# A new order for the first stage of a fused attention and MoE kernel: set-up products moved, C loaded without its zeros, the second weight tile sent for later

## The chip, the cores and the metric

The kernel runs on one core of one Trainium2 chip. The metric is the device time of one launch in microseconds (us), the median of several runs. TensorE (PE) multiplies matrices, VectorE (DVE), ScalarE (ACT) and GpSimd (POOL) work on elements, SyncE (SP) only starts transfers here. Each engine takes its instructions in the order in which the program wrote them; they wait for each other by semaphores.

## The reference

Three parts follow each other. First, a chunked linear attention over 4 batches, 8 heads, 768 positions, head size 32, state size 16:

```python
cum = np.cumsum(log_a, axis=-1)                 # per chunk of 32
L = np.exp(cum[..., :, None] - cum[..., None, :]) * causal
y_intra = einsum('bhij,bhjd->bhid', einsum('bhin,bhjn->bhij', C, B) * L, x)
y_inter = einsum('bhin,bhnd->bhid', C, state) * exp(cum)
state = exp(sum log_a) * state + sum_j B_j x_j exp(cum_end - cum_j)
```

Its output, 3072 tokens by 256, goes through a gated MLP (`silu(x @ w_gate) * (x @ w_val) @ w_out`, 1536 wide) and then through a routed MoE of 8 experts (256 to 1024 to 256, one expert for each token, with a gate).

## The kernel before

The attention is cut into 24 units (`NU`) of 128 positions by all 8 heads of a batch; four units make a block of 512 tokens. A product in full precision is made of three products of split operands (high by high, high by low, low by high), so most tensors have a high and a low half.

For a unit, `load(u)` (L160) sends for x, B and the transposed B in one tile (`xbb`, 256 KB) and for C in another (`cbd`, 256 KB, L170). The C tile is block diagonal over four heads: in each row three of four blocks of 64 columns are zeros, which come from memory with the rest. `weigh(u)` (L273) multiplies x by decays W; `scores_mm(u)` (L281) makes the state products (L291) and the scores (L297); `scores_m(u)` (L301, L305) masks the scores on VectorE; `states(u)` (L308) steps the running state on VectorE and ScalarE; `values_mm(u)` (L331) makes the outputs (L343, L353); `values_out(u)` (L357) multiplies them by the table `U` on VectorE and casts them on ScalarE into the high half of `xt` (L374); `values_low(u)` (L376) makes the low half (L380).

The decays are built once for each two blocks. `setup_ln` (L178) takes logarithms, `setup_decay` (L184, product `pw`) makes W, `setup_cum` (L189, product `pe`) makes `er`, `cum_split` (L218) splits it; `cum_ends_d`, `cum_ends` (L228, L236, product `pe2` with the table of ones `r16`) and `cum_store` make `eb`; `emit_d` (L249) spreads `er` into `du` on GpSimd (L259), and `emit_u` (L264) multiplies `du` by the table of ones `r32` (product `pu`, L270) and copies the result to `U` on ScalarE (L271). `setup_ones` (L213) casts the two tables from the constants `c1`.

The weights of the MLP come as 12 tiles (`load_w`, L387, 768 KB each, in three buffers, so that a tile can be sent for when the tile three before it has been read). They arrive as 64-bit floats and are decoded to a high half `wh` and a low half `wl` by `decode(f, ...)` (L396): parts 0 and "t" on ScalarE (L403, L406), "b" and "c" on VectorE (L412, L416), 2 on ScalarE (L419, `wh`), 3 on VectorE or GpSimd (L421, `wl`).

`first_block` (L807) writes the order of the first stage by hand, for all engines. After the set-up it runs units 0 to 3 in a loop, with pieces of decoding between them and `keep_busy` products (L199, L204), whose result nobody reads, behind each unit. Then a loop over i = 0 to 23 runs the MLP's products for the first two blocks (`mlp1_mm`, L430, 12 products of 128x512 for each i), with units 4 to 11 and the decoding of tiles 2 to 11 between them by two tables (`todo`, `units`). The first of these products needs all four units of block 0 and tile 0. The rest of the kernel is a loop over the further blocks with the routing, and the tiles of the experts.

SP's queue holds nearly all loads in program order: one that has to wait for its buffer holds up those behind it. The constants `c1` are sent for on ScalarE's queue.

## Time and profile before

| what | value |
|---|---|
| median of 3 runs | 530.3 us (530.1 to 530.32) |
| the profiled execution: its own time, its span | 530.17 us, 528.4 us |
| TensorE busy over the span | 505.0 us (96%), 4580 products |
| VectorE, ScalarE, GpSimd busy | 289.1, 219.5, 105.8 us |
| granted TensorE clock, mean | 0.989 |
| moved by DMA | 45.55 MB, mean 86 GB/s |

The span runs from the first to the last instruction. Busy times say how long an engine worked, not whether somebody waited for it; for that the chain of waits follows the work that ended last back to the start. The lines L... are those of the kernel before. In a timeline the bracket names how long the engine had been idle before an instruction, and what released it; "issue" stands for time in which it waited for nothing that the profile shows.

### The profile page before, as it was taken

How to read it: one execution, taken by the hardware profiler on the slowest of the kernel's cores; microseconds unless marked ns; L12 is line 12 of the kernel's file. 1: busy time of each engine (PE TensorE's matmuls, PEld its weight loads, DVE VectorE, ACT ScalarE, POOL GpSimd, SP SyncE). 2: the span in 40 equal slices, each digit the busy share in tenths (PEclk: the TensorE clock that was granted, in tenths of full speed). 3: DMA queues.
4: the chain of work that ended last, by engine and by line, in shares of the span. 5: the costliest groups of instructions: out<-in, count | busy, mean ns of one | idle time of the engine just before them, and what ended most of it. 6: DMA issues, size and time to landing. Idle time of an engine off the chain costs nothing.

```text
span 528.4 us, 11243 instructions
## 1 busy us (share of the span) xinstructions
PE 505.0 (96%) x4580; PEld 416.7 (79%) x4580; DVE 289.1 (55%) x631; ACT 219.5 (42%) x403; POOL 105.8 (20%) x127
## 2 busy tenths in 40 slices
PE   6889999999999999999999999999999999999990
PEld 3677787778788778888788778888899989999880
DVE  4998786944554544445444554455466564646320
ACT  4785575434333334233333332434454353534220
POOL 3200000220220130005000224211055426240220
PEclk9999999999999999999999999999999999999995
DMA  8954422011230312012100104234188544521100
GB/s 299 338 183 137 155 80 82 25 49 41 82 32 30 103 15 66 3 47 74 21 2 2 43 1 158 84 121 41 41 105 176 162 130 137 153 104 42 40 22 22
DMA packets 20694, 45.55 MB, mean 86 GB/s; under 512 B 4768, under 2 KB 8352, under 8 KB 20640
## 3 DMA queue, kind: packets, MB, share of 16 engines
q1 hardware_dynamic: 17424, 38.29, 26.2%
q0 software_dynamic: 3072, 6.41, 4.1%
q8 instruction: 37, 0.61, 0.6%
q14 instruction: 17, 0.14, 0.1%
q10 hardware_dynamic: 144, 0.11, 0.1%
HBM read 38.30 MB, written 6.50 MB: 85 GB/s over the span
## 4 chain that ended last, share of the span: by engine, by line
PE 76%; issue 11%; DVE 4%; POOL 3%; ACT 2%; DMA 1%; SPq 0%; POOLq 0%; DVEq 0%; ACTq 0%
PE py L469 19%; PE pg L441 18%; PE pv L441 18%; PE ph L758 7%; PE po L779 6%; PE pt L553 2%; POOL out L793 2%; PE pc L297 2%; PE py L353 1%; PE py L343 1%; PE pc L291 1%; DMA xbb<-in_xbb 1%; PE pu L270 1%; DVE wv L412 1%; PE px L747 1%
## 5 line engine op out<-in xcount | busy, mean ns | idle before, releaser
L441 PE MATMUL pg<-xt,wh 128*128 128x512 f32 x288 | 93.2, 404 | 0.3 <-ACT xt L374 0.2
L441 PE MATMUL pv<-xt,wh 128*128 128x512 f32 x288 | 90.4, 395 | 0.0
L449 DVE TENSOR_TENSOR h<-h,pv 128x512 f32<-128x512 f32 x72 | 49.4, 686 | 66.7 <-PE pv L441 55.6
L456 DVE TENSOR_TENSOR hl<-h,hh 128x512 fp32r<-128x512 f32 x72 | 50.2, 697 | 61.7 <-ACT hh L455 61.5
L758 PE MATMUL ph<-xt,hl 128*128 128x512 f32 x288 | 72.7, 394 | 0.0
L779 PE MATMUL po<-hl,hh 128*128 128x256 f32 x384 | 70.1, 283 | 0.0
L441 PEld LDWEIGHTS pv<-xt,wh 128*128 128x128 f32 x288 | 54.2, 188 | 12.8
L779 PEld LDWEIGHTS po<-hl,hh 128*128 128x128 f32 x384 | 60.3, 188 | 2.1
L455 ACT CAST hh<-h 128x512 fp32r<-128x512 f32 x72 | 44.6, 620 | 40.4 <-DVE h L449 40.4
L441 PEld LDWEIGHTS pg<-xt,wh 128*128 128x128 f32 x288 | 52.1, 188 | 11.6 <-ACT xt L374 0.6
L448 ACT ACTIVATE h<-pg 128x512 f32<-128x512 f32 x72 | 42.7, 593 | 41.7 <-PE pg L441 41.7
L614 POOL DMA_INDIRECT slots<-ids,si x24 | 26.0, 1081 | 168.4 <-DVE si L606 163.6
L758 PEld LDWEIGHTS ph<-xt,hl 128*128 128x128 f32 x288 | 51.7, 188 | 9.2
L469 PE MATMUL py<-hh,wh 128*128 128x512 f32 x144 | 58.7, 407 | 0.0
L441 PE MATMUL pg<-xt,wl 128*128 128x512 f32 x144 | 57.0, 396 | 0.3 <-DVE wl L421 0.3
L469 PE MATMUL py<-hl,wh 128*128 128x512 f32 x144 | 56.9, 395 | 0.0
L469 PE MATMUL py<-hh,wl 128*128 128x512 f32 x144 | 56.8, 394 | 0.0
L441 PE MATMUL pv<-xt,wl 128*128 128x512 f32 x144 | 56.8, 394 | 0.0
L779 PE MATMUL po<-hl,hl 128*128 128x256 f32 x192 | 53.9, 281 | 0.2 <-DVE hl L767 0.2
L767 DVE SCALAR_TENSOR_TENSOR hl<-ph,hh 128x512 fp32r<-128x512 f32 x48 | 33.0, 688 | 31.8 <-ACT hh L766 30.8
L766 ACT ACTIVATE hh<-ph 128x512 fp32r<-128x512 f32 x48 | 28.8, 600 | 41.4 <-PE ph L758 24.3
L779 PEld LDWEIGHTS po<-hl,hl 128*128 128x128 f32 x192 | 36.1, 188 | 0.4 <-DVE hl L767 0.4
(140 smaller groups left out, 669.6 us busy)
## 6 DMA issues: line engine op xcount, KB each, us to landing
eraw<-in_ew SPq DMA_DIRECT2D x24, 512.0 KB
wraw<-in_mw SPq DMA_DIRECT2D x12, 768.0 KB
xbb<-in_xbb SPq DMA_DIRECT2D x24, 256.0 KB
cbd<-in_cbd SPq DMA_DIRECT2D x24, 256.0 KB
yd<-yr SPq DMA_DIRECT2D x6, 528.0 KB
slots<-ids,si POOLq DMA_INDIRECT x24
xg<-yd,idx POOLq DMA_INDIRECT x24
out<-ob,idx POOLq DMA_INDIRECT x24
```

Source lines behind the costliest of these rows:

```text
L297: nc.tensor.matmul(out=r["pc"][g][32 * q:32 * q + 32, 0:256], lhsT=r["bt"][k, 32 * q:32 * q + 32], rhs=r["c"][k, q // 2].rearrange("p h i ...
L441: nc.tensor.matmul(out=t, lhsT=w[:, f, o:o + 128], rhs=xt[:, xp, k, cs], start=n == 0, stop=n == 5)
L448: nc.scalar.activation(out=h, in_=p[0], func=AF.Silu)
L449: nc.vector.tensor_tensor(out=h, in0=h, in1=p[1], op=ALU.mult)
L455: nc.scalar.copy(out=hh, in_=h)
L456: e.tensor_tensor(out=hl, in0=h, in1=hh.bitcast(F32), op=ALU.subtract)
L469: nc.tensor.matmul(out=yb[b][d][:, c:c + m], lhsT=w[:, f, o:o + 128], rhs=h, start=first and n == 0, stop=last and n == 2, skip_group_chec ...
L614: i = nc.gpsimd.indirect_dma_start(out=slots[0:E * upto], out_offset=bass.IndirectOffsetOnAxis(ap=si[:, s:s + 1], axis=0), in_=ids[g][:, o ...
L758: nc.tensor.matmul(out=p, lhsT=self.hl[:, w, o:o + 128], rhs=self.xt[:, xp, k], start=n == 0, stop=n == 5)
L766: nc.scalar.activation(out=hh, in_=p, func=AF.Relu)
L767: nc.vector.scalar_tensor_tensor(out=hl, in0=p, scalar=0.0, in1=hh.bitcast(F32), op0=ALU.max, op1=ALU.subtract)
L779: nc.tensor.matmul(out=self.po[s // 2][:, s % 2], lhsT=h[:, q], rhs=self.hl[:, w, o:o + DM], start=f == 0 and n == 0 and s % 2 == 0, stop= ...
```

## The change

C is loaded without half of its zeros: the rows of two heads are interleaved (`bk`, `bt`, C and the ones in `r16` get a new order), so that each row of a C tile needs only 256 of its 512 columns from memory. The tiles are four fixed buffers that GpSimd fills with zeros once, and each load writes two halves of 64 rows by 1 KB, in two transfers. The products read the tile with a stride; their number and size stay. In the first stage `setup_ones`, `cum_ends_d` and `emit_d(0)` come earlier; `warm_up` adds nine products of zeros in bf16 (five, two, two); the `keep_busy` products are 2, 2, 4, 4 instead of 0, 4, 4, 6. Unit 3's loads move to ScalarE's queue, behind `emit_u(0)`; the second weight tile is sent for behind unit 4, the third behind units 5 and 6. `emit_u(1)` moves from unit 0 to unit 2. The decoding of tiles 0, 1 and 2 is spread anew, tile 0's low half is made on VectorE instead of GpSimd, and unit 6's `weigh` comes before the MLP's loop.

```diff
--- before.py
+++ after.py
@@ -87,15 +87,16 @@
     at = inp["a"].reshape(NB * NH, NC, 128).reshape(NB, NH, NC, 128).transpose(3, 0, 2, 1)
     o["at"] = at.reshape(128, NBLK, 32)
     xk = inp["x"].reshape(NB, NH, NC, 128, D).transpose(3, 0, 2, 1, 4).reshape(128, NU, DM)
-    bk = inp["B"].reshape(NB, NH, NC, 128, N).transpose(3, 0, 2, 1, 4).reshape(128, NU, 128)
-    bt = inp["B"].reshape(NB, NH, NC, 128, N).transpose(1, 4, 0, 2, 3).reshape(128, NU, 128)
+    bq = inp["B"].reshape(NB, 4, 2, NC, 128, N)
+    bk = bq.transpose(4, 0, 3, 1, 5, 2).reshape(128, NU, 128)
+    bt = bq.transpose(1, 5, 2, 0, 3, 4).reshape(128, NU, 128)
     o["xbb"] = np.concatenate([xk, bk, bt], axis=2)
 
-    ct = inp["C"].reshape(NB, 2, 4, NC, 2, 64, N).transpose(1, 2, 6, 0, 3, 4, 5).reshape(2, 4, N, NU, 2, 64)
-    cd = np.zeros((2, 4, N, NU, 2, 4, 64), np.float32)
-    for h in range(4):
-        cd[:, h, :, :, :, h] = ct[:, h]
-    o["cbd"] = cd.reshape(128, NU, 512)
+    ct = inp["C"].reshape(NB, 2, 2, 2, NC, 128, N).transpose(1, 2, 6, 3, 0, 4, 5).reshape(2, 2, N, 2, NU, 128)
+    cd = np.zeros((2, 2, N, 2, NU, 2, 128), np.float32)
+    for p in range(2):
+        cd[:, p, :, :, :, p] = ct[:, p]
+    o["ct"] = cd.reshape(128, NU, 256)
     o["cst"] = _consts()
 
     def bits(w):
@@ -150,6 +151,7 @@
     r16 = ap_.tile([128, 128], F32R, name="r16")
     r32 = ap_.tile([128, 2, 128], F32R, name="r32")
     mk = c1[:, C_MK:C_MK + 64]
+    cbd = [ap_.tile([128, 4, 2, 64], F32, name=f"cbd{i}") for i in range(4)]
     raw = {}
     xt_t = {}
     y_t = {}
@@ -157,23 +159,34 @@
     v_t = {}
     s_t = {}
 
-    def load(u):
-        if u >= NU or u in raw:
-            return
-        r = {}
-        xbb = ap_.tile([128, 512], F32, name="xbb", tag="xbb", bufs=4)
-        nc.sync.dma_start(out=xbb, in_=I["xbb"][:, u])
-        r["x"] = xbb[:, 0:DM].rearrange("k (h d) -> k h d", h=8)
-        r["b"] = xbb[:, DM:DM + 128]
-        r["bt"] = xbb[:, DM + 128:]
-        r["c"] = ap_.tile([128, 2, 4, 64], F32, name="cbd", tag="cbd", bufs=4)
-        nc.sync.dma_start(out=r["c"].rearrange("p r h i -> p (r h i)"), in_=I["cbd"][:, u])
-        raw[u] = r
+    def load(*units, e=nc.sync, order=None):
+
+        t = []
+        for u in units:
+            if u >= NU or u in raw:
+                continue
+            r = raw[u] = {}
+            xbb = ap_.tile([128, 512], F32, name="xbb", tag="xbb", bufs=4)
+            r["x"] = xbb[:, 0:DM].rearrange("k (h d) -> k h d", h=8)
+            r["b"] = xbb[:, DM:DM + 128]
+            r["bt"] = xbb[:, DM + 128:]
+            r["c"] = cbd[u % 4]
+            t.append((xbb, I["xbb"][:, u]))
+            t.append((r["c"].rearrange("(r t) a c i -> t r (a c i)", t=2),
+                      I["ct"][:, u].rearrange("(r t) j -> t r j", t=2)))
+        for i in order or range(len(t)):
+            if i % 2:
+                for h in range(2):
+                    e.dma_start(out=t[i][0][h, :, 256 * h:256 * h + 256], in_=t[i][1][h])
+            else:
+                e.dma_start(out=t[i][0], in_=t[i][1])
 
     def setup_loads():
         nc.sync.dma_start(out=at0[:, 0:2], in_=I["at"][:, 0:2])
         nc.scalar.dma_start(out=c1, in_=I["cst"][:, 0:C1])
         nc.scalar.preload_act_table_set("natural_log_exp_and_others")
+        for t in cbd:
+            nc.gpsimd.memset(t, 0.0)
 
     def setup_ln(b0, b1):
         a = at[:, b0:b1]
@@ -205,14 +218,28 @@
                              rhs=r32.rearrange("p g j -> p (g j)").unsqueeze(1).to_broadcast([128, 2, 256]),
                              start=True, stop=True)
 
+    warm_t = []
+
+    def warm_up(n):
+
+        if not warm_t:
+            warm_t.append(ap_.tile([128, 128], BF16, name="zb"))
+            nc.vector.memset(warm_t[0], 0.0)
+            idle_t.append(ps.tile([128, 2, 256], F32, tag="y0", bufs=1, name="pi"))
+        for _ in range(n):
+            nc.tensor.matmul(out=idle_t[0].rearrange("p g j -> p (g j)").rearrange("p (n j) -> p n j", n=4),
+                             lhsT=warm_t[0], rhs=warm_t[0].unsqueeze(1).to_broadcast([128, 4, 128]),
+                             start=True, stop=True)
+
     def silu_first():
 
         t = ap_.tile([128, 1], F32, name="sf")
         nc.scalar.activation(out=t, in_=c1[:, C_ME:C_ME + 1], func=AF.Silu)
 
     def setup_ones():
+        p8 = c1[:, C_P8:C_P8 + 8].rearrange("p (q t) -> p q t", q=4).unsqueeze(2)
+        nc.vector.tensor_copy(out=r16.rearrange("p (q n t) -> p q n t", q=4, t=2), in_=p8.to_broadcast([128, 4, 16, 2]))
         p8 = c1[:, C_P8:C_P8 + 8].unsqueeze(2)
-        nc.vector.tensor_copy(out=r16.rearrange("p (h n) -> p h n", h=8), in_=p8.to_broadcast([128, 8, 16]))
         nc.vector.tensor_copy(out=r32.rearrange("p g (h i) -> p (g h) i", h=4), in_=p8.to_broadcast([128, 8, 32]))
 
     def cum_split(b0, n):
@@ -295,7 +322,7 @@
             for g in range(2):
                 k = slice(64 * g, 64 * g + 64)
                 nc.tensor.matmul(out=r["pc"][g][32 * q:32 * q + 32, 0:256], lhsT=r["bt"][k, 32 * q:32 * q + 32],
-                                 rhs=r["c"][k, q // 2].rearrange("p h i -> p (h i)"), start=True, stop=True,
+                                 rhs=r["c"][k, :, q // 2], start=True, stop=True,
                                  tile_position=(64 * g, 32 * q))
 
     def scores_m(u):
@@ -418,8 +445,8 @@
             elif part == 2:
                 nc.scalar.copy(out=wh[:, f], in_=wv_t[f].bitcast(F32))
             else:
-                low.tensor_tensor(out=wl[:, f], in0=wv_t.pop(f).bitcast(F32), in1=wh[:, f].bitcast(F32),
-                                  op=ALU.subtract)
+                nc.vector.tensor_tensor(out=wl[:, f], in0=wv_t.pop(f).bitcast(F32), in1=wh[:, f].bitcast(F32),
+                                        op=ALU.subtract)
 
 
     HALF = NF // 2
@@ -812,29 +839,33 @@
         nc.sync.dma_start(out=at0[:, 2:], in_=I["at"][:, 2:])
         load(2)
         load_w(0)
-        load(3)
-        load_w(1)
+        warm_up(5)
         setup_ln(0, 2)
+        setup_ones()
         setup_decay(0, 2)
         setup_cum(0, 1)
+        warm_up(2)
         weigh(0, nc.vector)
         scores_mm(0)
         cum_split(0, 1)
-        setup_ones()
+        p = cum_ends_d(0, 1)
+        d = emit_d(0)
         weigh(1, nc.gpsimd)
-        d = emit_d(0)
-        p = cum_ends(0, 1, cum_ends_d(0, 1))
+        p = cum_ends(0, 1, p)
+        warm_up(2)
         scores_m(0)
         cum_store(0, 1, p)
         states(0)
         emit_u(0, d)
+        load(3, e=nc.scalar)
         cum_pairs(1, 8)
         setup_ln(2, NBLK)
-        decode(0, 0)
         d = emit_d(1)
         weigh(2, nc.gpsimd)
         for u in range(4):
             scores_mm(u + 1)
+            if u == 2:
+                emit_u(1, d)
             values_mm(u)
             if u == 1:
                 setup_decay(2, NBLK)
@@ -842,38 +873,43 @@
             if u < 3:
                 scores_m(u + 1)
                 states(u + 1)
-            if u in (0, 2):
-                decode(u // 2, "t")
             values_out(u)
             if u == 0:
-                emit_u(1, d)
+                decode(0, 0, "t")
+            if u == 1:
                 decode(0, "b")
-            if u == 1:
+                decode(1, 0)
+            if u == 2:
                 decode(0, "c")
-            if u == 2:
+                decode(1, "t")
+                decode(0, 2)
+            if u == 3:
                 decode(1, "b")
-            keep_busy((0, 4, 4, 6)[u])
+                silu_first()
+            keep_busy((2, 2, 4, 4)[u])
             values_low(u)
-            load(u + 4)
             if u == 0:
+                load(4)
+                load_w(1)
                 weigh(3, nc.gpsimd)
             if u == 1:
+                weigh(4, nc.gpsimd)
+            if u == 2:
+                load(5, 6, order=(3, 0, 1, 2))
                 load_w(2)
+                weigh(5, nc.gpsimd)
+            if u == 3:
+                load(7)
+                decode(0, 3)
+                decode(2, 0)
                 load_w(3)
                 nc.sync.dma_start(out=c2, in_=I["cst"][:, C1:C_END])
-                weigh(4, nc.gpsimd)
-                decode(0, 2)
-                decode(0, 3, low=nc.gpsimd)
-                decode(1, 0)
-            if u == 2:
-                decode(1, "c")
-                silu_first()
-                decode(1, 2)
-                weigh(5, nc.gpsimd)
         scores_m(4)
         states(4)
+        decode(1, "c", 2)
+        weigh(6, nc.vector)
         decode(1, 3)
-        decode(2, 0, "t")
+        decode(2, "t")
         load_w(4)
 
         todo = {0: 2, 1: 3, 2: 4, 4: 5, 6: 6, 8: 7, 10: 8, 12: 9, 14: 10, 15: 11}
@@ -883,7 +919,7 @@
             b, f = q % 2, f + HALF * (q // 2)
             u = units.get(i)
             w = todo.get(i, NF)
-            if i + 1 in units and units[i + 1] > 4:
+            if i + 1 in units and units[i + 1] > 5:
                 weigh(units[i + 1] + 1, nc.vector if i < 16 else nc.gpsimd)
             if u == 7:
                 mlp1_down(*late.pop(0))
```

The diff leaves out the same index for C in `values_mm` (two places) and the parameter `low` in the head of `decode`.

## Rows read from the trace of the kernel before

**Rows 1.** Windows, core 0: bounds, length, busy us (instructions) by engine, clock, DMA share, GB/s.

```profile
10.91:27.68 16.77, 14.81 (x369) 10.34 (x359) 14.63 (x43) 13.05 (x27) 3.70 (x4) 1.00 0.92 334
27.68:53.48 25.80, 24.00 (x435) 18.53 (x434) 23.82 (x50) 17.02 (x29) 0.00 (x0) 1.00 0.48 162
53.48:520.00 466.52, 460.56 (x3705) 384.58 (x3705) 247.03 (x526) 185.98 (x341) 98.57 (x115) 1.00 0.27 70
```

**Rows 2.** Chain of waits, 14 to 54 us: start, us, what.

```profile
27.68 0.97 DVE wv L412
...
52.47 0.97 DVE wl L421
53.48 0.73 PE pg L441 x2
```

**Rows 3.** Timeline, first 11 us: start, duration, engine, instruction, idle before and its releaser.

```profile
0.73 0.40 ACTq L175 DMA_DIRECT2D c<-in_cst  x1
...
3.90 0.75 PE L193 MATMUL pe<-c,at 128*128 128x132 f32 x2
...
5.32 0.30 DVE L226 TENSOR_TENSOR er<-er,eh 128x132 f32<-128x132 f32 x1
...
6.61 0.61 POOL L278 TENSOR_TENSOR xw<-xbb,W 128x256 f32<-128x256 f32 x1 [6.17 <-DMA xbb<-in_xbb]
...
7.18 2.17 POOL L259 TENSOR_TENSOR du<-er,c 128x512 fp32r<-128x512 f32 x2
...
8.27 1.22 PE L270 MATMUL pu<-du,r 128*128 128x512 f32 x2 [1.60 <-POOL du L259]
...
9.43 0.47 PE L291 MATMUL pc<-xw,xbb 64*32 64x64 f32 x16
...
10.49 0.74 PE L343 MATMUL py<-mt,xw 64*32 64x64 f32 x31
...
10.91 0.76 DVE L305 TENSOR_TENSOR mt<-pc,c 128x256 f32<-128x256 f32 x2 [2.46 <-PE pc L297]
```

**Rows 4.** Timeline of TensorE, 12.4 to 21.3 us.

```profile
15.90 0.27 PE L186 MATMUL pw<-at,c 128*128 128x128 f32 x1 [0.85 <-issue]
...
16.37 1.16 PE L204 MATMUL pi<-r 128*128 128x512 f32 x4
17.46 0.34 PE L291 MATMUL pc<-xw,xbb 64*32 64x64 f32 x16
...
18.87 1.19 PE L204 MATMUL pi<-r 128*128 128x512 f32 x4
...
21.25 0.45 PE L297 MATMUL pc<-cbd,xbb 64*32 64x256 f32 x8 [0.91 <-issue]
```

**Rows 5.** Windows that count instructions of TensorE (PE, PEld).

```profile
3.41:12.57 9.16, 7.33 (x121) 4.09 (x121) 5.02 (x20) 3.22 (x9) 3.87 (x5) 1.00 1.02 360
3.41:15.05 11.64, 9.81 (x218) 5.98 (x219) 6.85 (x25) 5.34 (x12) 3.93 (x5) 1.00 1.00 361
15.90:20.12 4.22, 4.22 (x125) 3.14 (x125) 3.88 (x15) 3.74 (x10) 1.50 (x1) 1.00 1.02 338
```

**Rows 6.** DMA queues, 13.3 to 14.4 us: packets, MB, share of 16 engines.

```profile
q8 instruction: 1, 0.02, 5.3%
```

**Rows 7.** Groups of ScalarE by form, to 60 us: busy us, mean ns, idle before.

```profile
L403 ACT ACTIVATE ha<-wraw 128x768 f32<-128x768 f32 x8 | 7.3, 914 | 0.7 <-DMA wraw<-in_mw 0.7
...
L419 ACT CAST wh<-wv 128x768 fp32r<-128x768 f32 x6 | 5.0, 832 | 2.9 <-DVE wv L416 2.9
...
L271 ACT COPY U<-pu 128x512 f32<-128x512 f32 x4 | 2.1, 579 | 4.1 <-PE pu L270 4.1
...
L326 ACT ACTIVATE st<-se,eb 128x64 f32<-128x64 f32 x6 | 2.0, 340 | 0.0
```

**Rows 8.** Timeline of SP's queue, 29 to 30.9 us.

```profile
29.69 0.33 SPq L391 DMA_DIRECT2D wraw<-in_mw  x1
```

**Rows 9.** Windows behind that issue.

```profile
32.69:33.69 1.00, 0.00 (x0) 0.00 (x0) 1.00 (x5) 0.00 (x0) 0.00 (x0) 1.00 0.98 393
```

More of the change, by code (lines that the diff above doesn't have):

```diff
@@ L343, in values_mm @@
                     nc.tensor.matmul(out=py[i][32 * q:32 * q + 32, 128 * g:128 * g + 64], lhsT=r["xw"][k, 4 * g + q],
-                                     rhs=r["m"][k, g, q], start=g == 0, stop=True, tile_position=(64 * i, 32 * q),
+                                     rhs=r["m"][k, g, 2 * (q % 2) + q // 2], start=g == 0, stop=True, tile_position=(64 * i, 32 * q),
                                      skip_group_check=True)
@@ L353, in values_mm @@
                     nc.tensor.matmul(out=py[g][32 * q:32 * q + 32, o:o + 64],
-                                     lhsT=st[k, half, 32 * (q % 2):32 * (q % 2) + 32], rhs=r["c"][k, half, q],
+                                     lhsT=st[k, half, 32 * (q % 2):32 * (q % 2) + 32], rhs=r["c"][k, 2 * (q % 2) + q // 2, half],
                                      start=False, stop=True, tile_position=(64 * g, 32 * q), skip_group_check=True)
@@ L394, with decode @@
     ha_t = {}
-    def decode(f, *parts, low=nc.vector):
+    def decode(f, *parts):
         if f >= NF:
```

## The prediction

> **What bounds the kernel now.** I read the stages first [rows 1], then the chain of waits [rows 2], then the timeline of the first 21 us [rows 3, 4]. From 53.48 us on, TensorE is busy for 460.56 of 466.52 us, and the chain stays on it; nothing of that part changes. What can move is the moment at which that stretch begins. Before it the chain goes through VectorE and ScalarE: in 10.91 to 27.68 us VectorE is busy for 14.63 of 16.77 us, in 27.68 to 53.48 us for 23.82 of 25.80. I use one mark: 27.68 us, when VectorE begins to decode the third weight tile (`decode(2, "b")`, L412). From this mark the order of work on VectorE, TensorE and ScalarE is the same in both kernels. So I take the shift of the mark as the shift of the end.
>
> **The opening, up to `scores_m(1)`.** Now GpSimd waits for unit 1's x until 6.61, weighs it, and only then makes `du` from 7.18 on (two in 2.17, so 1.09 each); the u products follow at 8.27, and VectorE gets unit 1's scores at 10.91 [rows 3]. Moved ahead, `du` starts when the remainder `er` is there (5.32 + 0.30 = 5.62) and ends at 6.7. The product on it also needs `r32`; the two short copies of `setup_ones` now go to a time when VectorE waits for its first inputs, and cost nothing there as long as the constants are in when the first product uses them, ahead of 3.90. On TensorE the added zero products come in: five before any input is there (cover: TensorE has nothing to do before `pw`, just ahead of `pe` at 3.90), two after `pe` (3.90 + 0.5 = 4.40), two after the `pe2` product. A 512-column product takes 0.43 at the lower clock level (two `pu` in 1.22 with their drain) and 0.27 at the upper one (four in 1.09 from start to start) [rows 3, 4]. So: 4.40 + 0.86 = 5.26; unit 0's scores as unit 1's, 9.43 to 10.49, 1.06: 6.32; `pe2` 0.1; 0.86: 7.28. `du` has been ready since 6.7, so here the zero products cost up to 0.6 and `pu` is not what they protect. `pu` 0.7 to 0.86: 8.0; unit 1's scores 0.57 at the upper level or 1.06 at the lower, with 0.2 of drain: VectorE at 8.8 or at 9.4, against 10.91.
>
> **The clock.** [...] The bounds for the nine zero products are a loss of 0.9 (four of them in the path and no earlier rise) and a gain of 3 (all of 8.27 to 14.7 in half the time); most of the gain is swallowed by the waits below.
>
> **ScalarE.** The three loads of unit 3 now go out on ScalarE's queue after the `U` copies (two by 0.58 [rows 7], from 8.1 on). The one issue that ScalarE has made took 0.40 [rows 3], SP's take 0.33 later on [rows 8]; I take 0.40: 1.2. Behind them stand the second logarithm, unit 1's two states (0.34 each [rows 7]) and unit 0's cast, four short passes, some 1.3: 8.1 + 1.2 + 1.2 + 1.3 = 11.8, and VectorE's `values_low(0)` waits for that: it would be idle about 0.9 near 11. It has no worse follower: the freed `decode(0, "b")` comes only after unit 1.
>
> **VectorE's own sum.** From unit 1's scores to the mark it worked 14.63 us [rows 1]. Added: the low half of weight tile 0, which GpSimd did, 0.97 on VectorE as the row of another tile's [rows 2]. Idle: 0.9 as above and 0.3 for casts. 8.8 + 14.63 + 0.97 + 1.2 = 25.6.
>
> **TensorE's instruction pages.** TensorE stands still before 15.90 and before 21.25 with "issue" as the reason (0.85 and 0.91) [rows 4]. Up to the first stop it had run 218 products and 219 weight loads; between the stops 125 and 125 [rows 5]; with the semaphores that is about 256 instructions. One 16 KB instruction packet lies between 13.3 and 14.4 [rows 6], with the 16 DMA engines busy all the time (share 1.00 [rows 5]); work goes on 1.5 after it. So I read the stops as pages of instructions that come late because the transfers are in their way. The change shifts the first stop: nine products and nine weight loads more ahead of it, but four `pu` instructions fewer and the keep-busy ones at another place; it falls into the last products of unit 1. In the rows the page came 3.3 after 12.57, when TensorE had run 121 of each [rows 5]. That place is reached near 9.1 now; so the page is there at 12.5, while TensorE would be at the stop at 11.5: a stop of 1.0 stays. It may be none (the packet runs at once: 9.1 + 1.0 + 1.5 = 11.6) or 3 (it waits out the second weight tile).
> [...]
>
> **The third weight tile's landing.** SP's queue runs in order. `load(5, 6)` begins with unit 6's C, which needs the buffer that unit 2's products read. Their end: 12.5, rest of unit 1 0.25, `pw` and `pe` 0.47 (15.90 to 16.37), two keep-busy 0.55, unit 3's scores and unit 2's values 1.41 (17.46 to 18.87), `pu` 0.47: 15.7. Then six issues by 0.38 are ahead of `load_w(2)`: 18.0. The lone 786 KB of an issue at 29.69 are moved by about 33.3 (393 GB/s once it flows) [rows 8, 9]; with its receipt 4.0 to 5.0 from issue to use; I take 5.0, as small transfers stand ahead: 23.0. In the old order it is sent for a unit earlier and is long there. ScalarE's `decode(2, 0)` now waits for it, and behind it stand unit 4's two states (0.5) and `wh` of tile 1; then VectorE's `wl` of tile 1: 23.0 + 0.91 + 0.5 + 0.83 + 0.97 = 26.2 [rows 2, 7]. TensorE needs the states only after its first MLP tile (started about 20.5, held by `wl` of tile 0 until about 22, done near 24.3), so this wait is VectorE's. 26.2 is later than the 25.6 of the sum, so it sets the mark: 27.68 - 26.2 = 1.5 earlier.
>
> **Edits that I cost at nothing.** C without half its zeros: 131 KB less per unit, 0.33 at 393 GB/s; bounds 0 to 0.33 for each of the first four, but it is the order on GpSimd and TensorE that sets the opening, not the transfer; the extra issue on SP is counted above. The four zero fills on GpSimd: no such row here; between nothing and `du`'s 1.09 each they end before 5.0, and the first before C's first load is issued, the third one of SP's queue. The strided read of C: same columns, -0.1 to +0.1. Unit 3's x lands after 12, and its scores are not due before 13.3. `emit_u(1)` later: its first reader is unit 4.
>
> **Sum.** Profiled execution 530.17 (span 528.4 and 1.8 around it) - 1.5 = 528.67; the median of the runs is 0.13 above that execution: 528.8.
>
> **Rivals.**
> First, the pages are in time, as fewer bytes stand in their way: the stop is gone, the third weight tile lands a unit's wait earlier, and VectorE's own sum decides: mark 25.6, gain 2.1, 528.2. For it: a lull between the first and second weight tile. Against: both stops seen so far. [...]
> Second, the clock rises as late as now. For it: TensorE had worked with gaps since before 3.90, and no row before 15 is at the upper level. Then unit 1's values, `pw`, unit 3's scores and unit 2's values take longer: 1.06 for 0.57 in the scores and, at the same ratio, up to twice as long in the rest of the 1.41 of a unit, some 1.3 in all behind the stop: mark near 27.5, 530.1.
> Third, slower: the third weight tile is late. Place: ScalarE's `decode(2, 0)`. Price: one for one. It decides from a landing at 24.5 on (27.68 - 3.2), that is when the page comes after 14.0 instead of 12.5. For it: the page's packet would run after 11.5, into the second weight tile's transfer, and its wait, 0.8 in the rows (12.57 to 13.4), is then 3.2 long: page at 14.9, mark at 28.6, 531.2. Against: SP sends the second weight tile only after unit 4's C, so the packet has a lull near 10 to 12.
>
> **How the numbers follow.** Forecast 0.43, its own range 528.3 to 529.3; first rival 0.20; second 0.24; third 0.13. A measurement of this kernel tells 0.2%, 1.06 us, from no change: below 529.24 is faster, above 531.36 slower. Faster: the forecast, the first rival: 0.63. The third rival is slower than now but only by its later part over the bound: 0.10; the rest, 0.27, is no change that can be told. Range: the first rival's low side 527.6 up to 530.7, which leaves out the later part of the third rival and a fast case below.
>
> **What would show it.** Unit 1's scores on VectorE (L305, second pair) at 8.8; products at 0.27 per 512 columns by 8; one "issue" stop of about 1 near 11.5; ScalarE idle before `ha` of tile 2 until 23 with the DMA as releaser; `wl` of tile 0 on VectorE near 21; the mark at 26.2 and TensorE's stretch from about 52.0. It is wrong if the mark moves by less than 1, or if it moves and the stretch doesn't.

## The result and the profile after

The changed kernel takes 535.6 us (median of four runs, 535.32 to 537.37) where the kernel before took 530.3 in the same comparison: a ratio over all runs of 1.0107, 95% interval 1.0085 to 1.0129 (the medians alone give 1.0100). It is slower by 5.3 us; the forecast was 1.5 us faster, and the time lies outside the stated range. The profiled execution took 535.32, its span is 533.3 (528.4 before). The mark (VectorE's start on `decode(2, "b")`, 27.68 us before, 26.2 in the forecast) came at 31.43, the long stretch of TensorE at 57.60 instead of 53.48.

The stages answer to [rows 1]; three narrower windows follow, which the text below uses. Columns: bounds, length, then busy us and instructions of TensorE's products, its weight loads, VectorE, ScalarE and GpSimd, then granted clock, DMA share and GB/s.

```profile
10.91:31.43 20.52, 14.73 (x357) 9.68 (x350) 13.23 (x35) 12.38 (x24) 1.81 (x3) 0.92 0.64 231
31.43:57.60 26.17, 24.23 (x347) 18.50 (x347) 23.86 (x51) 16.98 (x29) 0.00 (x0) 0.93 0.50 169
57.60:533.30 475.70, 460.79 (x3705) 385.30 (x3705) 248.04 (x526) 185.86 (x341) 98.21 (x115) 0.99 0.25 65
...
4.00:9.50 5.50, 5.40 (x124) 3.01 (x123) 4.44 (x14) 1.74 (x5) 3.32 (x4) 1.00 0.77 202
14.90:18.30 3.40, 3.40 (x41) 1.94 (x40) 2.09 (x6) 2.27 (x6) 0.47 (x1) 0.51 0.02 9
14.90:19.70 4.80, 4.80 (x106) 2.88 (x105) 3.32 (x10) 3.17 (x8) 0.47 (x1) 0.64 0.03 10
```

From 10.91 to the mark VectorE works 13.23 of 20.52 us, where before it worked 14.63 of 16.77: it waits. The second stage is 0.37 longer than its counterpart of 25.80, the third 0.82 longer (475.70 against 528.36 - 53.48 = 474.88). So 3.75 us arise ahead of the mark, 0.37 behind it, 0.82 late in the long stretch: 4.94 of the 4.96 that the span grew.

SP's queue: start, duration, queue, line, transfer, number of issues. First four rows of the kernel before, then the changed kernel.

```profile
1.64 0.42 SPq L170 DMA_DIRECT2D cbd<-in_cbd  x1
2.10 0.46 SPq L165 DMA_DIRECT2D xbb<-in_xbb  x1
...
4.51 0.43 SPq L391 DMA_DIRECT2D wraw<-in_mw  x1
...
15.22 2.77 SPq L391 DMA_DIRECT2D wraw<-in_mw  x2
```

```profile
1.20 0.42 SPq L182 DMA_DIRECT2D xbb<-in_xbb  x1
1.66 1.19 SPq L180 DMA_DIRECT2D cbd<-in_ct  x2
2.90 0.59 SPq L182 DMA_DIRECT2D xbb<-in_xbb  x1
3.53 1.11 SPq L180 DMA_DIRECT2D cbd<-in_ct  x2
...
7.02 0.58 SPq L418 DMA_DIRECT2D wraw<-in_mw  x1
...
19.77 1.11 SPq L180 DMA_DIRECT2D cbd<-in_ct  x2
20.98 0.54 SPq L182 DMA_DIRECT2D xbb<-in_xbb  x1
21.56 1.12 SPq L180 DMA_DIRECT2D cbd<-in_ct  x2
22.78 1.07 SPq L182 DMA_DIRECT2D xbb<-in_xbb  x1
23.90 0.44 SPq L418 DMA_DIRECT2D wraw<-in_mw  x1
24.43 0.38 SPq L182 DMA_DIRECT2D xbb<-in_xbb  x1
```

In the first 27 us a pair of C halves (`cbd<-in_ct`, x2) holds SP for 1.11 to 1.27 us, where a whole C took 0.33 to 0.43 in most issues, and the next load takes 0.52 to 0.59 (once 1.07) instead of 0.33 to 0.46. The first weight tile (L418, 7.02) goes out 2.5 us later than the 4.51 of before, and the third one at 23.90 instead of 15.22, with 4.13 us of other issues ahead of it from 19.77 on. From 14.9 to 19.7 the 16 DMA engines are at a share of 0.03: hardly anything is under way, since SP stands before unit 6's C, which needs the buffer that unit 2's products read.

TensorE: the last column of a row is the idle time ahead of it and its releaser.

```profile
5.44 0.67 PE L324 MATMUL pc<-cbd,xbb 64*32 64x256 f32 x16
...
14.44 0.32 PE L380 MATMUL py<-cbd,st 64*32 64x64 f32 x9 [3.06 <-issue]
...
17.16 1.10 PE L324 MATMUL pc<-cbd,xbb 64*32 64x256 f32 x16
...
19.18 0.59 PE L380 MATMUL py<-cbd,st 64*32 64x64 f32 x32
...
20.97 0.66 PE L324 MATMUL pc<-cbd,xbb 64*32 64x256 f32 x16
...
257.19 0.45 PE L380 MATMUL py<-cbd,st 64*32 64x64 f32 x7 [0.49 <-issue]
```

The same 16 products take 0.67 at 5.44 (unit 0, already at the upper clock level), 1.10 at 17.16 and 0.66 at 20.97: behind a stop of 3.06 us, with "issue" as the reason (a page stop in what follows, as the prediction reads it), TensorE runs at the lower level (granted clock 0.51 in 14.9 to 18.3). Unit 2's products end at 19.8. The last row is called the late pause: from the first product of this unit (255.29) to the next product of the MLP (257.57) 2.28 us pass, where 1.39 passed before (251.34 to 252.73).

ScalarE and VectorE ahead of the mark.

```profile
28.41 0.91 ACT L430 ACTIVATE ha<-wraw 128x768 f32<-128x768 f32 x1 [3.22 <-DMA wraw<-in_mw]
...
29.71 0.81 ACT L446 CAST wh<-wv 128x768 fp32r<-128x768 f32 x1
```

```profile
8.55 0.74 DVE L332 TENSOR_TENSOR mt<-pc,c 128x256 f32<-128x256 f32 x2
...
30.56 0.96 DVE L448 TENSOR_TENSOR wl<-wv,wh 128x768 fp32r<-128x768 f32 x1 [2.87 <-ACT wh L446]
31.43 0.95 DVE L439 SCALAR_TENSOR_TENSOR wv<-ha,wv 128x768 int32<-128x768 int32 x1
```

ScalarE stands for 3.22 us before `ha` of the third weight tile, `wh` of the second is queued behind it, and VectorE's `wl` waits 2.87 for that.

### The profile page after: what moved, and what is told of

The parts are those of the page before. It is cut to its first block, busy times and chain, and to the rows that moved or that the text cites. A ratio compares the mean times of both kernels' runs of the same rounds, so it can differ in the third digit from the quotient of the medians.

```text
span 533.3 us, 11327 instructions
## 1 busy us (share of the span) xinstructions
PE 509.3 (95%) x4587; PEld 418.7 (78%) x4587; DVE 291.2 (55%) x633; ACT 219.7 (41%) x403; POOL 105.5 (20%) x130
## 4 chain that ended last, share of the span: by engine, by line
PE 80%; issue 9%; DMA 3%; DVE 2%; POOL 2%; SPq 1%; ACT 1%; POOLq 0%; DVEq 0%
PE py L496 18%; PE pg L468 18%; PE pv L468 18%; PE ph L785 8%; PE po L806 8%; PE pt L580 2%; PE pc L324 2%; PE py L380 1%; POOL out L820 1%; PE py L370 1%; DMA wraw<-in_mw 1%; PE pc L318 1%; PE px L774 1%; SPq L180 1%; PE pu L297 1%
```

## The experiments

Each is the changed kernel with the edit shown, unless it says "the kernel before with". Ratios are to the kernel before on the same chip (530.4 to 530.6 us), over all runs, with 95% intervals; rows come from one execution of each kernel.

**1. The third weight tile sent a unit earlier.**

```diff
             if u == 1:
+                load_w(2)
                 weigh(4, nc.gpsimd)
 ...
                 load(5, 6, order=(3, 0, 1, 2))
-                load_w(2)
```

> The changed kernel with one load moved back: the third weight tile is sent for behind the second (unit 1 of the loop) instead of behind units 5 and 6. Theory (the tile is late, 28.4 us instead of 23 at ScalarE's decode, and VectorE's mark at 31.4 follows): ScalarE's decode of tile 2 waits for nothing, the mark falls from 31.4 to about 29, TensorE does not idle at 30.2 to 31.9 and keeps the upper clock there; 532 to 533 us against 535.6. The page rival (what costs is the 3 us stop at 11.4 and the clock lost after it): stop unchanged, less than 1 us gained, 534.6 or more.

534.22 us, 1.0084 [1.0048, 1.0119]. The wait for the third tile is gone and the mark is at 28.62, 2.8 earlier, but only some 1.4 us reach the end (expected were 2.6 and more, and the interval overlaps that of the changed kernel): the next tile is late in its place.

```profile
30.34 0.90 ACT L430 ACTIVATE ha<-wraw 128x768 f32<-128x768 f32 x1 [1.28 <-DMA wraw<-in_mw]
```

It was sent at 25.33, behind three more pairs of C halves, and the late pause is there as well (0.90 before 255.65), 0.5 us longer than in the changed kernel.

**2. C whole again, with its zero half, in one transfer.**

```diff
-                for h in range(2):
-                    e.dma_start(out=t[i][0][h, :, 256 * h:256 * h + 256], in_=t[i][1][h])
+            e.dma_start(out=t[i][0], in_=t[i][1])      # 128 rows of 2 KB
```

> The changed kernel with C stored with all its zeros and loaded in one transfer of 128 rows by 2 KB; the fills stay, nothing else differs. Theory that the two half transfers are what makes SP's queue slow (1.1 to 1.2 us for a pair and 0.5 to 1.1 for the load behind it, where a whole one took 0.4): the first weight tile is sent for at about 5 instead of 7.0, the third about 2 us earlier than 23.9; 533 us or less. Rival (the wait for unit 2's products at the head of that queue, not the issues): the third tile moves by less than 0.5 and the time by less than 1 us. Rival bytes: 131 KB more per unit make the first weight tile land later, and the kernel slower than 535.6.

532.92 us, 1.0036 [1.0017, 1.0055]: more than half of the loss comes back. Each C takes SP 0.33 to 0.43, and the opening moves more bytes than with half of them:

```profile
4.00:9.50 5.50, 5.50 (x124) 3.05 (x124) 4.26 (x14) 2.23 (x6) 3.33 (x4) 1.00 1.01 349
14.90:18.30 3.40, 3.40 (x104) 2.04 (x103) 3.06 (x11) 2.97 (x8) 0.00 (x0) 1.00 0.04 12
```

```profile
13.77 0.32 PE L378 MATMUL py<-cbd,st 64*32 64x64 f32 x8 [2.38 <-issue]
...
16.98 0.59 PE L378 MATMUL py<-cbd,st 64*32 64x64 f32 x32
```

349 GB/s where the changed kernel moves 202, and in this execution (531.73 us) the clock holds behind the stop (1.00 in 14.9 to 18.3). The third tile goes out at 19.43 instead of 23.90. It is still late: ScalarE waits 3.32 for it until 26.29, and the mark is at 29.30. Of the 4.47 us by which the tile goes out earlier only 2.12 reach ScalarE: from issue to use it takes 6.86 instead of 4.51, with the DMA engines at a share of 0.97 in between (0.89 in the changed kernel).

**3. The kernel before with half of C alone** (fills, layout and the two half transfers; order of loads, set-up and decodes as before).

> The kernel before with nothing but the new C: fills, new order of rows, two half transfers per unit, all in the old order of work. If the half transfers cost by their issues, slower than 530.3 by 0.5 to 2 us (the first weight tile and unit 3 are sent for later); if fewer bytes pay, 529.5 or less; if neither, within 0.5 us of it.

534.48 us, 1.0072 [1.0052, 1.0092]. This one edit, which the forecast cost at nothing, loses 3.9 us, more than the 0.5 to 2 that I expected. Its pair of issues takes the same time, and the third weight tile still goes out early, at 14.79:

```profile
1.68 1.19 SPq L180 DMA_DIRECT2D cbd<-in_ct  x2
2.91 0.59 SPq L182 DMA_DIRECT2D xbb<-in_xbb  x1
...
13.63 1.11 SPq L180 DMA_DIRECT2D cbd<-in_ct  x2
14.79 4.08 SPq L405 DMA_DIRECT2D wraw<-in_mw  x2
```

In its trace the shift is 1.3 us at 53 us, and some 2 more come with a pause near 255 us (1.12 before 254.92).

**4. The kernel before with the set-up order alone** (ones, end products and `du` ahead of unit 1).

> The kernel before with only the set-up order of the change: the tables of ones, the spread ends and du ahead, no zero products, all loads and decoding as before. du starts at 5.7 instead of 7.2, unit 1's scores reach VectorE near 9.5 instead of 10.9. If VectorE's sum decides, 1 to 1.4 us faster, 529 us; if the page stop before 15.9 stays where it is in time and holds TensorE, less than 0.5 us.

530.64 us, 0.9993 [0.9975, 1.0010]: unit 1 comes earlier (its scores reach VectorE at 9.51) and nothing of it reaches the end; the mark is at 27.73. The 1.4 us are first lost in a wait for the first weight tile, which lands no earlier than before; so `decode(0, "b")` on VectorE starts where it started. Two rows of this kernel, then the same two of the kernel before:

```profile
11.35 0.94 ACT L403 ACTIVATE ha<-wraw 128x768 f32<-128x768 f32 x1 [2.26 <-DMA wraw<-in_mw]
...
13.59 0.96 DVE L412 SCALAR_TENSOR_TENSOR wv<-ha,wv 128x768 int32<-128x768 int32 x1 [2.16 <-ACT wv L406]
```

```profile
11.24 0.92 ACT L403 ACTIVATE ha<-wraw 128x768 f32<-128x768 f32 x1 [0.75 <-DMA wraw<-in_mw]
...
13.47 0.96 DVE L412 SCALAR_TENSOR_TENSOR wv<-ha,wv 128x768 int32<-128x768 int32 x1 [0.65 <-ACT wv L406]
```

TensorE's second page stop is 1.56 long instead of 0.91.

**5. C whole, and the third and fourth weight tiles early** (edits 1 and 2, and `load_w(3)` from unit 2, behind `load(5, 6)`).

```diff
                 load(5, 6, order=(3, 0, 1, 2))
+                load_w(3)
```

> The changed kernel with C whole in one transfer (as in the run that sent it whole, 532.9 us) and, besides, the third weight tile sent from unit 1 and the fourth from unit 2, ahead of unit 7's loads. Theory: what is left of the loss with C whole (+2.3 us) is the two weight tiles that land late; then SP sends the third tile before 16 and the fourth before 22, ScalarE's two decodes of them wait for nothing, VectorE's mark is at 26.5 to 27.5 (27.68 before), and the time is 529.5 to 530.5. Rival: what is left is the page stop of 2.4 near 12 us and the clock that is lost behind the next pause; then the weights come in time, TensorE still pauses over 1.5 us ahead of 30 us and runs 3.4 us at the low clock, and the time stays at 531.8 to 533.

531.04 us, 1.0012 [1.0001, 1.0024]; the profiled execution took 530.03, the mark is at 27.51. Neither of the two tiles is waited for (`ha` of the third at 23.07); for the second ScalarE waits 0.82. So halves of C and late weight tiles are the loss, to within 0.6 us; what the forecast promised on top is not there.

```profile
9.30:27.51 18.21, 15.11 (x350) 10.09 (x340) 15.65 (x43) 13.61 (x28) 2.61 (x3) 0.92 0.89 302
```

```profile
13.72 0.32 PE L378 MATMUL py<-cbd,st 64*32 64x64 f32 x8 [1.64 <-issue]
```

From unit 1's scores to the mark VectorE works 15.65 us, which is the forecast's 14.63 + 0.97, and idles 2.56, where the forecast had 1.2: 0.80 behind the page stop, 1.22 in three waits for ScalarE, the rest in short ones.

**6 and 7. Which price of the half transfers is it?** Once one transfer of 128 rows of 1 KB, once two blocks of 64 neighbouring rows. Both leave half of C's rows in the wrong columns, so they test the transfers and are no kernels to use.

```diff
-            t.append((r["c"].rearrange("(r t) a c i -> t r (a c i)", t=2), ...
+            t.append((r["c"][:, 0:2].rearrange("p a c i -> p (a c i)"), I["ct"][:, u]))      # 6
+            t.append((r["c"].rearrange("(t r) a c i -> t r (a c i)", t=2), ...                # 7
```

> The changed kernel with the half-width C in a single transfer of 128 rows of 1 KB; so the half that belongs into the second columns of each odd row lies in the first columns, and the values of these heads are computed from wrong places. Theory: the loss is in the number and shape of the issues on SP, not in the bytes; then each C takes SP 0.33 to 0.43 as a whole one does, the first weight tile goes out near 4.5, the third near 19.4 (23.90 in the changed kernel), TensorE has one wait less per unit and no stop near 255 us, and the time is 532.3 to 533.2. Rival: SP is slow because of what stands ahead (the fills of the four C buffers, the waits on them); then the third tile still goes out after 22 and the time stays above 534.5.

> The changed kernel with its two half transfers of C as two blocks of 64 neighbouring rows instead of every second row; half of the C rows lie in the wrong columns, and the values of these heads are computed from wrong places. Theory: each issue has a price of its own and the stride of two rows adds to it; with neighbouring rows the pair costs 0.7 to 0.85 us on SP, the third weight tile goes out near 21.5, and the time is 534 to 534.8 with the stop near 255 us still there (it hangs on the extra wait per unit on TensorE). Rival: the price is of 64-row transfers whatever their stride; then the pair still takes 1.1 to 1.27, the third tile goes out near 23.9, and the time is 535.2 to 536.

The single transfer: 532.63 us, 1.0039 [1.0027, 1.0052], as fast as C whole. SP takes 0.33 to 0.43 for it and sends the first weight tile at 4.48. So it is the second issue, not the bytes; but the halved bytes gain nothing either, and the third tile went out only at 22.40, as the stop was 2.98 with the low clock behind it (0.54 granted in 14.9 to 18.3) and a load ahead of the tile held SP for 1.38 (in an execution of 534.25, above the median). The row blocks: 538.70 us, 1.0164 [1.0147, 1.0181], with the pair at the same price:

```profile
1.66 1.20 SPq L180 DMA_DIRECT2D cbd<-in_ct  x2
2.90 0.59 SPq L182 DMA_DIRECT2D xbb<-in_xbb  x1
```

The stride cost nothing here (1.20 without it, 1.19 with it); a pair of 64-row transfers does. I had put this kernel at 534 to 536: its opening is that of the changed kernel (mark 31.55), and of the 2.3 us between the two profiled spans 1.4 are a longer late pause, here in two parts, and 0.6 are there when the long stretch begins (58.21 for 57.60).

```profile
258.43 0.40 PE L380 MATMUL py<-cbd,st 64*32 64x64 f32 x14 [1.20 <-issue]
...
260.11 0.48 PE L496 MATMUL py<-hl,wh 128*128 128x512 f32 x1 [0.62 <-issue]
```

**8. The kernel before with the set-up order and the nine zero products.**

> The kernel before with the new order of the set-up (ones, the end products, du ahead of unit 1) and the nine zero products; C whole, loads, weight tiles and decodes in the old order. Theory: the early clock makes unit 1 to 3 shorter, and as the weight tiles still come in the old order the gain of the opening reaches the mark: clock at the upper level from about 5 us, mark 0.8 to 1.5 before 27.68, time 529.0 to 529.8. Rival: the opening runs into the first page stop earlier and waits longer there, and the clock is lost again after it, as with the set-up order alone (530.64); then the mark stays within 0.4 of 27.68 and the time is 530.3 to 531.

531.11 us, 1.0013 [1.0004, 1.0023]. Nearer the rival, and past its bounds: unit 1's scores come early (9.16), then VectorE waits 2.59 for ScalarE, which waits 2.00 for the first weight tile, there are two stops of 1.47 and 1.62 (0.85 and 0.91 in [rows 4]), the clock is low from 14.4 to 17.8 (four products of 128x512 take 1.81 at 16.38, 1.19 at 19.52), and the mark is at 28.65.

**9. The changed kernel without the zero products** (`warm_up(5)` and both `warm_up(2)` taken out).

> The changed kernel without its nine zero products. Theory: they raise the clock early (4.7 us), but unit 1 then runs into the page stop and waits there, so the early clock is worth nothing at the end; without them the clock rises near 11.5, the stop falls 18 instructions later in the order of work and lasts under 2.2, the third weight tile goes out within 0.7 of 23.90, and the time is 535 to 536. Rival: the early clock is worth the 1.3 us that the forecast gave it; then the time is 536.6 to 537.2.

536.89 us, 1.0134 [1.0093, 1.0174], in the rival's range, but its interval overlaps that of the changed kernel: the zero products gain about a microsecond here or nothing. The stop is 1.98 before 14.60, and the third tile goes out at 21.66, earlier than with them, but ScalarE has it only at 29.23 (28.41 with them).

**10 to 12. Is it the request or the transfers that make the page late?** 56 products of 32 rows and 32 columns in place of the first five, in the kernel of experiment 5 (10) and in the changed kernel (11); and experiment 5 with the first weight tile sent behind unit 4's loads (12).

```diff
-        warm_up(5)
+        page_fill(56)     # matmul(idle_t[0][0:32, 0, 0:32], zb[:, 0:32], zb[:, 0:32])
```

> The kernel with C whole and both weight tiles early (531.0 us, first page stop 1.64, work on at 13.72), with its first five zero products of 512 columns replaced by 56 of 32 rows and 32 columns: 102 more instructions on TensorE before any input is there. Theory: a page of instructions is asked for when TensorE enters the page before it, and takes some 5 us from then to work (10.78 to 15.90 before, 8.99 to 13.72 in this kernel, 8.22 to 14.44 in the changed one); with 102 instructions more the entry lies near 5.5 instead of 8.99, the packet near 8.5, and the stop falls among unit 1's first products at about 9 to 10.5 and lasts under 0.7; TensorE is at the products of unit 2 a good 1.5 us earlier, the mark at 26 to 26.8, the time 529 to 530. Rival: the page comes at 11.3 or later whenever it is asked for, as the weight tile's transfer stands before it; then the stop only moves ahead in the order of work, is as long or longer (2 to 3.5 us), and the time is 531 to 532.5.

> The changed kernel with the same replacement: 56 small zero products for its first five. Theory (the page's time runs from the entry into the page before): the stop of 3.06 near 11.4 becomes one of under 1.2 near 10, work goes on before 12.5 (14.44), SP sends the third weight tile near 22 instead of 23.90, and the time is 533 to 534.3. Rival (the page waits for the transfers): work goes on no earlier than 14, the third tile is sent at 23.5 to 24.5, and the time is 535 to 536.5.

> The kernel with C whole and both weight tiles early (531.0 us), but with the first weight tile sent only behind unit 4's loads, after unit 0's products of the values, near 10 us instead of 4.5. Theory: the first page's packet (11.28) waits behind the first weight tile's 768 KB; without them it starts within 1.5 us of the entry near 9, work goes on by 12, and the stop is under 0.5. Rival: the page has a time of its own from the entry on; then the packet still starts at 11 to 12 and the stop is 1.5 to 2.5. The time itself is no test, since the first tile's decode is late in either case (531 to 535).

538.57 us, 1.0162 [1.0144, 1.0180]; 540.80 us, 1.0208 [1.0184, 1.0232]; and, for 12, a single run of 532.06. The theory's forecasts are near for the first stop, and wrong for the time. In 10 the first packet of instructions starts at 9.67 instead of 11.28 and the first stop is gone; the next one, a page later, is longer than all before:

```profile
19.15 0.33 PE L375 MATMUL py<-mt,xw 64*32 64x64 f32 x4 [3.10 <-issue]
```

The clock is low from 18.7 to 25.5 (16 score products take 1.10 at 22.19, 0.64 at 8.88), and TensorE has later waits for VectorE too (2.29 before 159.50, 0.77 before 265.77). In 11 the packet comes at 7.97 and no page stop is left there; what is late instead is GpSimd's `xw`, which waits for x until 16.09 (3.58 of TensorE's time before 17.48), and the third tile goes out at 24.04. Its late pause is the longest (1.90 and 0.70 before 261.66 and 262.71). In 12 the packet starts at 9.86 and the stop is 0.82, not under 0.5; ScalarE waits for the late tile and TensorE 2.72 for ScalarE's exponential. So both are true: more instructions run ahead (1.6 us in 10, 3.9 in 11) and fewer bytes sent ahead (1.4 in 12) bring the packet forward. No trace shows the request itself; that a page is asked for on entering the one before it is the theory's assumption. At all 18 page stops in the first 25 us of the traces work goes on 2.2 to 2.6 us after a packet's start (13.40 to 15.90 before, 11.89 to 14.44 after).

**13. The first weight tile and its decode a unit later** (experiment 12, and ScalarE's and VectorE's parts of `decode(0)` in units 1 and 2).

> The kernel with C whole and both weight tiles early (531.0 us), with the first weight tile sent behind unit 4's loads and its decode one unit later on ScalarE and VectorE. Theory: the first page packet then starts near 9.9 and the stop is about 0.8 instead of 1.64, ScalarE no longer waits for this tile ahead of the exponential (2.72 us of TensorE's time when only the transfer was moved), the mark is at 26.3 to 27.2, and the time 529.3 to 530.2, below the kernel before. Rival: VectorE has nothing to do while the first tile is late and has its decode to do when the others stand in line; then the mark is at 27.7 or later and the time 530.5 to 532.

531.57 us, 1.0017 [1.0008, 1.0026]: the rival. The first stop is 0.16, the second has grown to 2.56, the mark is at 30.11.

```profile
13.23 0.32 PE L378 MATMUL py<-cbd,st 64*32 64x64 f32 x8 [0.16 <-issue]
...
20.98 0.34 PE L316 MATMUL pc<-xw,xbb 64*32 64x64 f32 x5 [2.56 <-issue]
```

**14 and 15. Where the late pause comes from:** C whole from unit 8 on and in halves before, and the reverse.

```diff
+            if u >= 8:      # 14; u < 8 in 15
+                t.append((r["c"].rearrange("p a c i -> p (a c i)"), I["cf"][:, u]))
+                continue
```

> The changed kernel with C whole, in one transfer, from unit 8 on, and in two halves for units 0 to 7 as it was. Theory: the pause near 255 us comes from the later units' own half transfers (a wait more in TensorE's stream, or SP's time); then it is gone, the opening stays as it was (third weight tile sent near 23.9, mark near 31.4), and the time is 533.8 to 535. Rival: the pause comes from where the opening has put TensorE; then it stays at 0.7 to 2.3 us, and the time is 535.3 to 536.5.

> The counterpart: C whole for units 0 to 7 and in two halves from unit 8 on. Theory (later units' halves make the pause): the opening as with C whole (third weight tile sent near 19.4, mark near 29.3), the pause near 255 us there again with 0.7 to 2.3 us, the time 533.5 to 535. Rival (the opening makes it): no pause, 532.5 to 533.2.

534.86 us, 1.0088 [1.0071, 1.0105], and 532.53 us, 1.0044 [1.0028, 1.0059]. The pause is in neither trace. So neither theory holds alone: of the 17 traces, the pause stands in the six with two half transfers throughout (the changed kernel, 1, 3, 7, 9, 11) and in none of the others. The count of TensorE's instructions does not tell them apart: up to the unit's first product the traces have 2702 products and as many weight loads without it and with it (2 and 7; semaphore instructions are not in this count). A packet of instructions that takes some 3 us lies next to the pause (3.50 from 256.81 on in the changed kernel), but in kernels without it too (3.02 from 254.35 on in 2). Its cause stays open; it is worth 0.9 us in the changed kernel's trace and up to 3.4 in others. 15 agrees with C whole everywhere (532.92): the loss of the half transfers that can be explained lies in the opening.

## Why the prediction was wrong

**Right: the opening.** VectorE has unit 1's scores at 8.55 (8.8 forecast, 10.91 before); the three loads hold ScalarE's queue until 9.29 (10.5 by the forecast's 8.1 + 1.2 + 1.2); the upper clock level comes by 5.44 already (by 8 in the forecast). That the forecast took 8.8, with the upper level there for unit 1's scores, and not 9.4 was an estimate that no trace of the kernel before shows; in the changed kernel's these 16 products take 0.67 at 7.72, where they took 1.10 at 9.64 before. None of it was worth anything at the end (experiments 4 and 8, where the first weight tile, which the forecast does not price, is waited for instead).

**Wrong, first: the size of the page stop.** The forecast had TensorE at the stop at 11.5 and off again at 12.5; it was there at 11.38 and off at 14.44. The 3.06 us are the upper bound that I had named and not taken. I had let the page's time run from an instruction in unit 1's products, "3.3 after 12.57"; the packet starts at 13.40 in the kernel before and only 1.5 us earlier in the changed one, although TensorE is 3.7 earlier at the stop (11.38 for 15.05, [rows 4]). A faster opening thus turned into a longer stop. The kernels with a shorter opening show page stops of up to 3.1 us, but for experiment 11, where GpSimd was late first. What sets the moment of the packet the forecast did not know; experiments 10 to 12 show that instructions run ahead and bytes sent ahead both move it.

**Wrong, second: the clock behind the stop.** The forecast let unit 2's products end 3.2 us after the stop, at the upper level. They took 5.33, as TensorE went back to the lower level after its pause (granted clock 0.51). In experiment 2, where the clock held, the same products took 3.80 (13.77 to 17.57): some 1.5 of the 2.13 us go with the lost clock, and the forecast's 3.2 was 0.6 short at the upper level too. I had weighed a clock that rises late, and not one that is lost again.

**Wrong, third: SP's price for a half transfer.** "Six issues by 0.38" were 2.3 us; they took 4.13. I had taken the price of whole C rows for halves, and "the extra issue on SP is counted above" was counted at that price. The same price sits in the opening, where it sends the first weight tile 2.5 us later: experiment 3 shows 3.9 us for an edit that I had put between a gain of 0.33 each and nothing.

**The sum, with measured terms.** Mark 26.2 forecast; stop +1.94 (14.44 for 12.5); unit 2's products +2.13 (5.33 for 3.2); issues +1.83 (4.13 for 2.3); landing -0.49 (23.90 to 28.41 is 4.51, for 5.0); ScalarE and VectorE behind it -0.18 (3.02 for 3.2): 31.43, as measured. The terms are not independent: in experiment 2 the four issues ahead of the tile take 1.80, and the landing takes 6.86. Nor was the tile alone from which the forecast read its 4.0 to 5.0: SP sent x at 30.11 and C at 30.59 behind it, and their bytes are in [rows 9] too. The rule "shift of the mark is shift of the end" gave 3.75 of 4.96; the rest is the fourth weight tile (ScalarE waits 0.94 for it before 32.74), a lost clock from 32.0 to 35.4 (0.50 granted), and the late pause.

**The third rival was the mechanism**, at its place and with its price: "it decides from a landing at 24.5 on", one for one; with the landing at 28.41 it gives a mark of 31.6. I gave it 0.13 and a page at 14.9; the page came at 14.4, and what carried it further were the two terms that it did not have. Its counterargument, a lull near 10 to 12, failed: SP sent the second weight tile at 10.27, before the packet of 11.89, and the DMA engines were at a share of 0.97 to 1.04 from 10 to 12.

**A term put at nothing that the stop hid: unit 3's x.** It was to land after 12, with its scores not due before 13.3. GpSimd had it at 14.18, after 5.08 us of waiting. Behind the stop this cost nothing; with the stop of the forecast the scores would have been due at 13.8, and in experiment 11, without the stop, TensorE waits 3.58 for it.

**Where the forecast gain went.** With the late tiles and the halves gone (experiment 5), VectorE's sum is as forecast, but it begins 0.5 later (9.3 for 8.8) and waits 1.4 us more: a mark of 27.51 for 25.6. Where experiment 5's first stop of 1.64 was shortened most, a second one appeared (0 and 3.10 in 10; 0.16 and 2.56 in 13). I take it that the opening is paced by TensorE's pages of instructions and by the first weight tile, both under full transfers; that is read from the pattern, and no run without the transfers shows it. No version tried beats the kernel before.

## What to carry to other kernels

Price a changed transfer by its number of issues and rows, from the queue's own rows, and then price everything that stands behind it in the same queue: here 0.7 us more per C moved a weight tile on which ScalarE, then VectorE, then TensorE stood waiting. Before shortening an opening, look in it for "issue" stops and for waits on transfers that will land no earlier: time won ahead of one came back here as a longer wait (3.06 for 0.85), or as the next (0 and 3.10 in experiment 10), and the clock was lost behind some stops (0.51 granted in the changed kernel, 1.00 in experiment 2). A large transfer that needs no buffer should not stand behind a small one that does: `load_w(2)` sent a unit earlier took the wait of 3.22 us away.

## What was not expected of the hardware

Here a transfer of 64 rows of 1 KB took SP mostly 0.47 to 0.60 us to issue, whether the 64 rows were neighbours or every second, and one of 128 rows of 1 or 2 KB mostly 0.33 to 0.43; the load behind a pair mostly took 0.52 to 0.59 in the opening. With half of C's bytes in two transfers the DMA engines moved 202 GB/s in 4 to 9.5 us at a share of 0.77, in one transfer 245 at 0.92, and with all bytes in one transfer 349 at a share of 1. And of two kernels with nearly equal openings (marks 31.43 and 31.55) one is 3.1 us slower at the median, and most of what its trace locates is a pause 225 us later.
